# Pooled attention and a gated conv FFN: conv on two blocks without copies of h, keys loaded in pairs

## The chip, the cores and the metric

The kernel runs on one core of a Trainium2 chip. The metric is the device time of one launch in microseconds; beside it stands the profile of one execution. Engines are named as in the profile: PE (TensorE), PEld (its weight loads), DVE (VectorE), ACT (ScalarE), POOL (GpSimd), SP (SyncE, which only issues DMAs here).

## The reference

Eight batches b, each with 8 heads, 576 positions and head size 64. Keys and values are averaged over groups of 8 positions, so that each head attends to 72 pooled keys. The result feeds a feed-forward layer with a depthwise convolution over positions (3 taps) as a gate.

```
k_p = k.reshape(B, H, 72, 8, 64).mean(axis=3)         # v_p likewise
scores = q @ k_p.T / 8;  attn = softmax(scores)
x = (attn @ v_p) as (B, 576, 512)
h = max(x @ w_in, 0)                                  # (B, 576, 1024)
conv_out[s] = sum over k of conv_w[k] * h[s + k - 1]  # per channel, zeros outside
out = (h * sigmoid(conv_out)) @ w_out                 # (B, 576, 512)
```

## The kernel before

Batches go in four groups g of two. A group has 9 tiles t of 128 rows: four of its first batch, one shared (t = 4, 64 rows of each), four of the second.

Keys of a batch are loaded by `load_k` into one of three `kp` buffers, f32 in HBM and bf16 on the chip, with 9 neighbouring positions in a partition. `prep_k` pools and transposes them at once on PE: 36 matmuls against the pooling matrix `pm` (L469), or 72 in 64x64 tiles (L479); `copy_k` (L494) brings them to `kT`. q is transposed (L533, or L537 in 64x64 tiles) and copied to `qT` (L543). Values are loaded with 8 positions side by side in a partition; DVE adds halves three times (L503) and spreads the sum into `vm` times a head mask (L507).

A tile of attention is: scores (L585, or L572 in 64x64 tiles), row maximum on DVE (L598), the shift by it on PE (L618, first group) or DVE (L610, later groups, into `sd`), exp on ACT (L636), transposition to `eT` on PE (L647, copied at L661) or by DMA (L656, from the third group on), values (L672), quotient on DVE (L685, L687) to `x`, and transposition to `xT` on PE (L704, L712) or by DMA (L696, from batch 4 on).

The feed-forward part of a batch is: `w_in` (L738 by tiles for batch 0, L717 for the others), relu on ACT to `hT` (L748, L726), the convolution, tanh on ACT to `tg` (L815), `ffn_gate` on DVE (tg + 1 at L825, times h at L826, to `gT`), `w_out` on PE (L833), a copy to `osb` (L844) and two stores on SP's queue (L856).

The convolution is on PE as matmuls with diagonal 64x64 matrices `dw`, one for each tap, block of 128 channels `fb` and half of the block. To use all four 64x64 quarters of the array, row half r computes positions half r, and both output halves c are wanted of it. Where r and c differ, the data must lie in the other half of the partitions, so `ffn_swap` (L783) copies each pair of blocks of h with its halves exchanged into `hX`, on DVE or ACT, and `dw` holds the exchanged matrices too:

```
rhs=hT[r * D:(r + 1) * D, fb, src:src + hi - lo] if r == c
else hX[r * D:(r + 1) * D, fb % 2, src:src + hi - lo],
```

The order is not written by hand. `Graph` holds every step with an estimate of its duration on each engine that may do it, a key (a number that says how urgent it is), and the buffers that it uses; `Graph.order` plans all engines in time and emits the steps in the order of their planned starts. Each engine then runs its own instructions strictly in that order. PSUM's 8 banks are handed out in the plan, singly or in pairs. Loads are issued on POOL's queue, with at most eight in flight; the instruction that builds the identity `ident`, the pooling matrix `pm` and the head mask stand in the same queue. While PE would be idle, the plan puts in `fill` matmuls on a blank tile (L462).

Of the kernel before, what the change touches and what calls it, by code (L numbers as in the profile page):

```python
# [33 lines left out]
class Graph:  # L34
# [8 lines left out]
    STAY = 111.55  # L43
    LAZY = 1.11
# [5 lines left out]
    ATT = 39.8  # L50
    SPREAD = -183.35
    PREP_K = -29.07
    PREP_Q = 51.67
    PREP_V = 749.64
    GATE = 126.95
    CONV = 47.63
    SWAP = 261.14
    QCONV = -325.78
    OUT = 297.24
    LAST = 982.97  # L60
    FIRST = 196.4
    V0 = 281.91
    DW = 1007.11
# [3 lines left out]
    SWAP_DVE = 8  # L67
    BANKS = 8
    URGENT = -857.49
    NUDGE = {  # L70
        ('a', 0): -37.24, ('a', 1): 86.29, ('a', 2): -5.89, ('a', 3): -182.14, ('a', 4): -71.88, ('a', 5): -38.08,
        ('a', 6): -16.5, ('a', 7): 33.86, ('f', 0): -74.2, ('f', 1): -24.97, ('f', 2): -93.38, ('f', 3): 5.65,
        ('f', 4): 184.26, ('f', 5): -74.62, ('f', 6): -30.32, ('f', 7): -60.28, ('k', 0): 43.83, ('k', 1): -32.07,
        ('k', 2): 116.54, ('k', 3): 96.98, ('k', 4): 76.61, ('k', 5): 198.93, ('k', 6): -180.13, ('k', 7): 37.1,
        ('l', 'ident'): -61.73, ('l', 'k0'): -86.22, ('l', 'k0+'): -94.89, ('l', 'k1'): 2.95, ('l', 'k2'): 53.08, ('l', 'k3'): 66.15,
        ('l', 'mask'): -87.39, ('l', 'out'): 38.13, ('l', 'pm'): 4.15, ('l', 'q0'): -15.29, ('l', 'q0+'): 17.25, ('l', 'q1'): 12.42,
        ('l', 'q2'): 15.71, ('l', 'q3'): 88.03, ('l', 'v0'): -16.64, ('l', 'v1'): 37.82, ('l', 'v2'): -93.85, ('l', 'w0'): 36.34,
        ('l', 'w1'): 32.89, ('o', 0): 10.16, ('o', 1): -176.32, ('o', 2): 53.61, ('o', 3): 23.03, ('o', 4): -220.0,
        ('o', 5): -20.99, ('o', 6): -27.22, ('o', 7): 235.82, ('q', 0): -151.91, ('q', 1): 69.49, ('q', 2): -38.42,
        ('q', 3): 125.71, ('q', 4): 44.96, ('q', 5): 180.73, ('q', 6): 184.91, ('q', 7): 145.41, ('v', 0): -44.02,  # L80
        ('v', 1): -24.54, ('v', 2): 24.37, ('v', 3): 282.98, ('v', 4): -72.92, ('v', 5): -239.89, ('v', 6): -128.0,
        ('v', 7): -32.56,
# [14 lines left out]
    def order(self):  # L97
# [18 lines left out]
        def room(o):  # L116
            t, need = 0.0, 0
            new = {}
            for k in o.uses:
                if k.slots is not None:  # L120
                    continue
                if k.ring == "ps":
                    need += k.n
                    continue
                n = new[k.ring] = new.get(k.ring, 0) + 1
                q = taken[k.ring]
                if len(q) + n > self.rings[k.ring]:
                    f = idle_from(q[n - 1 - self.rings[k.ring]])
                    if f is None:
                        return None  # L130
                    t = max(t, f)
            if need:
                f = place(need)
                if f is None:
                    return None
                t = max(t, f[0])
            return t

        def place(n):
# [6 lines left out]
            return min(c, default=None)  # L146

# [32 lines left out]
        while avail:  # L180
# [56 lines left out]
            if o.land is not None:  # L237
                fixed, size, rate = o.land
                if size:
                    wire = max(wire, s + d + 0.3) + size / rate  # L240
                    o.end = wire + fixed
                    landings += [o.end] * o.dmas
                else:
# [24 lines left out]
def kernel(  # L268
# [17 lines left out]
    C = 9  # L286
# [14 lines left out]
             "hT": 2, "gT": 2, "xT": 2, "qT": 3, "kp": 3, "qp": 2, "hX": 3, "v": 2, "vm": 5, "kT": 5, "sd": 3, "r": 3, "s": 2}  # L301
# [8 lines left out]
    def banks(token):  # L310
# [6 lines left out]
    mask = const.tile([P, NJ, 3], BF16, name="mask")  # L317
    warm = const.tile([P, 2], FP32, name="warm")
# [3 lines left out]
    cw_raw = const.tile([3 * n_fb, 3 * D], FP32, name="cw_raw")  # L322
    convw = const.tile([P, 2, 3 * n_fb], FP32, name="convw")
    ident_2 = const.tile([P, D], BF16, name="ident_2")
    dw = const.tile([P, 2, 3 * n_fb, D], BF16, name="dw")
    shapes = {
        "qp": ([P, H // 2, S], BF16), "kp": ([P, H // 2, S], BF16), "qT": ([P, 2, 2, S], BF16),
# [4 lines left out]
        "hX": ([P, 2, S], BF16),  # L332
# [5 lines left out]
    def buf(*key):  # L338
        return buffers[key[0]][tokens[key].slots[0]]

# [17 lines left out]

    def load_q(b, **part):
        load_heads(buf("qp", b), q, b, **part)  # L360

    def load_k(b, **part):
        load_heads(buf("kp", b), k, b, **part)
# [9 lines left out]
    def load_conv():  # L373
        cw = moe_conv_w.rearrange("k (fb p) -> (k fb) p", p=P)
        nc.sync.dma_start(out=cw_raw[:, 0:P], in_=cw)
        nc.sync.dma_start(out=cw_raw[:, P:P + D], in_=cw[:, 0:D])
# [58 lines left out]

    def turn_conv_weights(ps):
        cps = bank(ps)[:, 0:6 * n_fb].rearrange("p (x j) -> p x j", x=2)
        for x in range(2):
            nc.tensor.transpose(
                out=cps[:, x, :],  # L440
                in_=cw_raw[:, x * D:x * D + P],
                identity=ident_f[0:3 * n_fb, 0:3 * n_fb],
            )

    def build_conv_matrices(part, ps=None, act=False):
        if part == 0:
            nc.vector.tensor_scalar(
                out=convw, in0=bank(ps)[:, 0:6 * n_fb].rearrange("p (x j) -> p x j", x=2), scalar1=2.0, scalar2=None, op0=OP.mult
# [3 lines left out]
        x, n = (part - 1) // 2, 3 * n_fb // 2  # L452
        todo = slice((part - 1) % 2 * n, (part - 1) % 2 * n + n)
        nc.vector.tensor_tensor(
            out=dw[:, x, todo],
            in0=ident_2.unsqueeze(1).to_broadcast([P, n, D]),
            in1=convw[:, x, todo].unsqueeze(2).to_broadcast([P, n, D]),
# [6 lines left out]
    def prep_k(b, half, ps, mode):  # L464
        for c in range(C):
            for hh in range(2):
                k_rows = buf("kp", b)[:, 2 * half + hh, c * D:(c + 1) * D]
# [30 lines left out]

    def prep_v(b, step):
        vt = buf("v", b)  # L500
        if step < 3:
# [8 lines left out]
            in1=mask.unsqueeze(3).to_broadcast([P, NJ, 3, D]),  # L510
# [271 lines left out]
    def ffn_swap(b, f2, r, copy):  # L782
        copy(  # L783
            out=buf("hX", b, f2)[r * D:(r + 1) * D, :, :],
            in_=buf("hT", b)[(1 - r) * D:(2 - r) * D, 2 * f2:2 * f2 + 2, :],
        )

    def ffn_conv(b, fb, ps):
        g, i = where[b]
        hT, hX = buf("hT", b), buf("hX", b, fb // 2)  # L790
        cps = banks(ps)
# [5 lines left out]
        for n in range(max(map(len, todo))):  # L797
            for r in range(2):
                for c in range(2):
                    if n >= len(todo[r]):  # L800
                        continue
                    tap, lo, hi, src = todo[r][n]
                    nc.tensor.matmul(  # L803
                        out=cps[c * D:(c + 1) * D, r, lo:hi],
                        lhsT=dw[r * D:(r + 1) * D, int(r != c), tap * n_fb + fb, :],
                        rhs=hT[r * D:(r + 1) * D, fb, src:src + hi - lo] if r == c
                        else hX[r * D:(r + 1) * D, fb % 2, src:src + hi - lo],
                        start=(n == 0),
                        stop=(n == len(todo[r]) - 1),
                        skip_group_check=True,  # L810
                    )
# [10 lines left out]
    def ffn_gate(b, fb):  # L822
        g, i = where[b]
        tg = buf("tg", b, fb)
        nc.vector.tensor_scalar(out=tg, in0=tg, scalar1=1.0, scalar2=None, op0=OP.add)  # L825
        nc.vector.tensor_tensor(  # L826
            out=buf("gT", g)[:, fb, i * S:(i + 1) * S], in0=tg, in1=buf("hT", b)[:, fb, :], op=OP.mult
        )
# [17 lines left out]
    def ffn_store(g, t, queue, only=None):  # L846
        osb = buf("osb", g, t)
        if t == 4:
            blocks = [(b, C - 1) for b in groups[g]]
        elif t < 4:  # L850
            blocks = [(groups[g][0], 2 * t), (groups[g][0], 2 * t + 1)]
        else:
            blocks = [(groups[g][1], 2 * t - 10), (groups[g][1], 2 * t - 9)]
        for j, (b, c) in enumerate(blocks):
            if only in (None, j):
                queue.dma_start(  # L856
                    out=out[b].rearrange("(p c) d -> c p d", c=C)[c],
                    in_=osb[j * TB:(j + 1) * TB, :],
                )
# [41 lines left out]
    kp, qp, qTt = {}, {}, {}  # L901
    kb = B and H * S * D * 4

    def add_load(kind, b, key, share=1.0, **part):
        f, ring, toks = (load_k, "kp", kp) if kind == "k" else (load_q, "qp", qp)
        if b not in toks:
            toks[b] = token(ring, b)
# [7 lines left out]
    def add_load_v(b, key):  # L915
# [6 lines left out]
             "k2", "q2", "v2", "k3", "q3"]  # L922
# [7 lines left out]
    cwl = add({"SP": 1.1}, soon(), load_conv, land=(1.5, 0, 1))  # L930
# [19 lines left out]
    hmc = add({"DVE": 0.5}, soon(), build_mask_columns, after=[hm])  # L950
    dw0 = add({"DVE": 0.2}, soon(), lambda: build_conv_matrices(0, cwtok), after=[cwp], uses=[cwtok])
    dwo = [add({"DVE": 1.0}, START + Graph.DW + n, lambda n=n: build_conv_matrices(n), after=[dw0]) for n in (1, 2, 3, 4)]
    win = [add({"POOL": 0.6}, first("w%d" % j), lambda j=j: load_w_in(j), land=(0.8, 2 * P * d_ff * 4, RATE)) for j in range(2)]
    wout = add({"POOL": 0.9}, first("out"), load_w_out, land=(LATE, d_ff * d_model * 4, RATE))
    for b in (1, 2, 3):
        add_load("k", b, first("k%d" % b))
        add_load("q", b, first("q%d" % b))
        add_load_v(b, first("v%d" % b) if b < 3 else -20)
    for b in range(4, B):
        w = (b - 4) * SLOTS  # L960
        add_load("k", b, w - 2)
        add_load("q", b, w - 1)
        add_load_v(b, w)
# [7 lines left out]

    def add_prep(b, key_k, key_q, gap):
        key_k, key_q = key_k + nudge("k", b), key_q + nudge("q", b)
# [220 lines left out]
```

## Time and profile before

| | us |
|---|---|
| median of 3 runs | 244.89 |
| lowest, highest | 244.22, 246.25 |
| profiled execution, span from first to last instruction | 244.0 |
| PE busy | 220.9 |
| PEld busy | 154.3 |
| DVE busy | 182.0 |
| ACT busy | 168.3 |
| POOL busy | 29.1 |

The profile is one execution; the span leaves out what lies before its first and after its last instruction. Busy time counts an engine once where its instructions overlap, so the sum over instructions of their mean duration is larger than the busy time. Matmuls overlap each other, and a matmul's own duration says little on the pace of many: the distance between neighbours does. A row of a group of instructions names line, engine, operation, tiles and shape, then the count, the busy time and the mean duration in ns, then idle time just before it and what ended it. A row of a stretch gives its bounds and length, the busy time and count of PE, PEld, DVE, ACT and POOL, the granted clock, the DMA share and GB/s. A row of the chain of waits gives start, duration and what ran.

### The profile page before, as it was taken

To read this page: it belongs to the slowest core of one execution; us is meant where nothing else is said; L and a number is where in the kernel's file an instruction comes from. 1 tells how busy PE (TensorE), PEld (TensorE's weight loads), DVE (VectorE), ACT (ScalarE), POOL (GpSimd) and SP (SyncE) were. 2 spreads that over 40 slices of the span, in tenths; PEclk is the share of its full clock that TensorE was granted. 3 is DMA by queue.
4 is the path that set the end of the run, shared out by engine and by line. 5 is a ranking of instruction groups with operands and counts; after the bars stand their busy time and mean duration, and the time that the engine had idled before them with its cause. 6 is when DMAs were issued, how large, how long until landed. Compare 5 with 4: busy or idle time off the path is not lost.

```text
span 244.0 us, 7852 instructions
## 1 busy us (share of the span) xinstructions
PE 220.9 (91%) x3354; PEld 154.3 (63%) x3377; DVE 182.0 (75%) x398; ACT 168.3 (69%) x264; POOL 29.1 (12%) x48
## 2 busy tenths in 40 slices
PE   6568998998999999999999996979999999899991
PEld 2446986876675676678775554757655576676440
DVE  7667648899999999999999995755799413956301
ACT  2254764599996876498998654949966386989330
POOL 7942223200122020220010000000000000000000
PEclk9999999999999999999999999999999999999998
DMA  5999999999189958697208568593216577400356
GB/s 81 164 205 207 207 208 208 207 207 202 22 141 185 197 83 190 104 179 153 46 3 141 126 134 91 107 139 89 24 46 149 109 137 167 117 3 6 84 137 164
DMA packets 43707, 31.53 MB, mean 129 GB/s; under 512 B 23680, under 2 KB 39064, under 8 KB 43672
## 3 DMA queue, kind: packets, MB, share of 16 engines
q0 software_dynamic: 15952, 16.26, 42.2%
q1 hardware_dynamic: 27640, 14.64, 29.5%
q8 instruction: 26, 0.43, 0.7%
q10 hardware_dynamic: 80, 0.13, 0.2%
q14 instruction: 9, 0.07, 0.1%
HBM read 32.52 MB, written 9.44 MB: 172 GB/s over the span
## 4 chain that ended last, share of the span: by engine, by line
PE 51%; DVE 26%; ACT 8%; DMA 7%; issue 5%; POOL 0%; SPq 0%; DVEq 0%; ACTq 0%; POOLq 0%
PE psum L833 16%; PE psum L717 14%; PE psum L803 7%; DVE negm L598 5%; DVE gT L826 4%; PE psum L672 3%; DVE sd L610 3%; DMA kp<-in_k_dram 3%; PE psum L738 3%; DVE tg L825 2%; ACT hT L726 2%; DVE hX L783 2%; DVE x L687 2%; DVE v L503 2%; DMA eT<-e 2%
## 5 line engine op out<-in xcount | busy, mean ns | idle before, releaser
L833 PE MATMUL psum<-w_out_sb,gT 128*128 128x512 bf16 x266 | 66.6, 379 | 2.0 <-issue 0.8
L717 PE MATMUL psum<-xT,w_in_sb 128*128 128x288 bf16 x448 | 61.1, 286 | 2.0 <-DMA xT<-x 1.3
L717 PEld LDWEIGHTS <-w_in_sb 128*128 128x128 bf16 x448 | 41.8, 98 | 15.4 <-DMA xT<-x 1.6
L833 PEld LDWEIGHTS <-gT 128*128 128x128 bf16 x288 | 26.0, 98 | 25.9 <-issue 0.7
L815 ACT ACTIVATE tg<-psum 128x576 bf16<-128x576 f32 x64 | 37.8, 655 | 3.0 <-PE psum L803 2.5
L726 ACT ACTIVATE hT<-psum 128x576 bf16<-128x576 f32 x56 | 34.4, 648 | 7.5 <-PE psum L717 7.1
L844 ACT COPY osb<-psum 128x512 f32<-128x512 f32 (+1 forms) x31 | 17.9, 579 | 24.5 <-PE psum L833 23.3
L783 DVE COPY hX<-hT 64x1152 bf16<-64x1152 bf16 x41 | 18.7, 458 | 18.3 <-ACT hT L726 15.4
L803 PE MATMUL psum<-hT,dw 64*64 64x224 bf16 (+3 forms) x576 | 30.9, 246 | 0.8 <-ACT tg L815 0.7
L803 PEld LDWEIGHTS <-dw 64*64 64x64 bf16 x1152 | 24.7, 107 | 10.5 <-issue 9.5
L826 DVE TENSOR_TENSOR gT<-tg,hT 128x576 bf16<-128x576 bf16 x64 | 29.3, 458 | 2.2
L803 PE MATMUL psum<-hX,dw 64*64 64x288 bf16 (+3 forms) x576 | 30.7, 246 | 0.0
L598 DVE TENSOR_REDUCE negm<-psum 128x8 f32<-128x576 f32 (+1 forms) x36 | 25.9, 750 | 2.4 <-PE psum L585 2.2
L783 ACT COPY hX<-hT 64x1152 bf16<-64x1152 bf16 x23 | 26.4, 1150 | 0.5
L687 DVE TENSOR_TENSOR x<-psum,r 128x512 bf16<-128x512 f32 x36 | 24.9, 692 | 1.2
L636 ACT ACTIVATE e<-sd 128x576 bf16<-128x576 f32 x27 | 18.2, 682 | 8.1 <-DVE sd L610 6.7
L672 PE MATMUL psum<-vm,eT 128*128 128x130 bf16 (+5 forms) x240 | 18.5, 222 | 4.2 <-DMA eT<-e 2.2
L825 DVE TENSOR_SCALAR tg<-tg 128x576 bf16<-128x576 bf16 x64 | 19.4, 304 | 3.4 <-ACT tg L815 3.2
L672 PEld LDWEIGHTS <-eT 128*128 128x128 bf16 (+1 forms) x240 | 14.7, 100 | 9.4 <-issue 3.0
L610 DVE TENSOR_TENSOR sd<-psum,negm 128x576 f32<-128x576 f32 x27 | 19.6, 749 | 0.1
L685 DVE RECIPROCAL r<-psum 128x8 f32<-128x8 f32 x36 | 7.3, 201 | 8.8 <-PE psum L672 8.7
L543 ACT COPY qT<-psum 128x1152 bf16<-128x1152 bf16 (+2 forms) x11 | 10.7, 992 | 4.2 <-PE psum L533 4.1
(67 smaller groups left out, 227.9 us busy)
## 6 DMA issues: line engine op xcount, KB each, us to landing
out_dram<-osb SPq DMA_DIRECT2D x71, 128.0 KB, 2.4
v<-in_v_dram POOLq DMA_DIRECT2D x8, 512.0 KB, 8.8
kp<-in_k_dram POOLq DMA_DIRECT2D x7, 576.0 KB, 16.0
qp<-in_q_dram POOLq DMA_DIRECT2D x7, 576.0 KB, 12.5
w_in_sb<-in_moe_w_in_dram POOLq DMA_DIRECT2D x2, 512.0 KB, 14.7
w_out_sb<-in_moe_w_out_dram POOLq DMA_DIRECT2D x1, 1024.0 KB, 20.0
kp<-in_k_dram POOLq DMA_DIRECT2D x2, 288.0 KB, 5.4
v<-in_v_dram POOLq DMA_DIRECT2D x8, 64.0 KB, 8.4
```

Of the source, the lines that this page charges most:

```text
L598: nc.vector.tensor_reduce(out=a["m"][0:rows], in_=a["s"][0:rows, :, 0:2 * KW].rearrange("p a (h s) -> p a h s", s=Sp), axis=AX.X, op=OP.ma ...
L610: nc.vector.tensor_tensor(out=a["d"][0:rows], in0=a["s"][0:rows, :, 0:2 * KW].rearrange("p a (h s) -> p a h s", s=Sp), in1=a["m"][0:rows]. ...
L672: nc.tensor.matmul(out=a["o"][lo:hi, h // 4, (h % 4) * (D + 1):(h % 4 + x1 - x0) * (D + 1)], lhsT=a["eT"][:, j, lo:hi], rhs=buf("vm", b)[: ...
L687: nc.vector.tensor_tensor(out=a["x"][0:rows].rearrange("p (a h d) -> p a h d", a=2, d=D), in0=ov[:, :, :, 0:D], in1=r[0:rows].unsqueeze(3) ...
L717: nc.tensor.matmul(out=banks(ps)[:, j, 0:SC], lhsT=w_in_block(dc, fb), rhs=buf("xT", g)[:, dc, i * S + j * SC:i * S + (j + 1) * SC], start ...
L726: nc.scalar.activation(out=buf("hT", b)[:, fb, :].rearrange("p (a s) -> p a s", a=2), in_=banks(ps)[:, :, 0:SC], func=ACT.Relu, scale=0.5,)
L783: copy(out=buf("hX", b, f2)[r * D:(r + 1) * D, :, :], in_=buf("hT", b)[(1 - r) * D:(2 - r) * D, 2 * f2:2 * f2 + 2, :],)
L803: nc.tensor.matmul(out=cps[c * D:(c + 1) * D, r, lo:hi], lhsT=dw[r * D:(r + 1) * D, int(r != c), tap * n_fb + fb, :], rhs=hT[r * D:(r + 1) ...
L815: nc.scalar.activation(out=tg.rearrange("p (a s) -> p a s", a=2), in_=banks(ps)[:, :, 0:SC], func=ACT.Tanh, scale=0.5,)
L825: nc.vector.tensor_scalar(out=tg, in0=tg, scalar1=1.0, scalar2=None, op0=OP.add)
L826: nc.vector.tensor_tensor(out=buf("gT", g)[:, fb, i * S:(i + 1) * S], in0=tg, in1=buf("hT", b)[:, fb, :], op=OP.mult)
L833: nc.tensor.matmul(out=bank(ps)[0:rows, :], lhsT=buf("gT", g)[:, fb, t * P:t * P + rows], rhs=w_out_sb[:, fb, :], start=(fb == 0), stop=(f ...
```

## The change

Convolution: one step now does two blocks `fb` = 2 f2 and 2 f2 + 1. Quarter (r, c) of the array works on block 2 f2 + (r ^ c), so all data come from `hT` as it lies; `hX`, `ffn_swap` and the exchanged half of `dw` are gone. Output half c of an odd block then holds the other half's channels, and the two halves change places when DVE adds 1 to tanh, in two instructions of 64 partitions. A step needs two pairs of PSUM banks at once (`two_pairs` in `Graph.order`).

Keys of batches 2 to 7: both batches of a group come by one load of 4608 neighbouring elements for each partition, DVE adds halves three times as for v, and 18 matmuls against a selection matrix `pick` transpose the sums of both batches. There is one buffer `kk` for keys, also for those of batches 0 and 1.

Stores: one DMA for each tile, except the last tile. The mask for `vm` is widened once to 64 equal columns. The conv weights need one load and one transposition, and two products instead of four. All keys of the plan (the constants of `Graph` and `NUDGE`) have other values, the loads at the start among them, so that the order of all engines' instructions is another one.

```
-             ... "qT": 3, "kp": 3, "qp": 2, "hX": 3, "v": 2, ...
+             ... "qT": 3, "kk": 1, "qp": 2, "v": 2, ...
...
-    dw = const.tile([P, 2, 3 * n_fb, D], BF16, name="dw")
+    dw = const.tile([P, 3 * n_fb, D], BF16, name="dw")
...
+    def load_pair(g):
+        rows = k[groups[g][0]:groups[g][1] + 1].rearrange("b h s d -> (b h s) d").rearrange("(p r) d -> p (r d)", p=P)
+        nc.gpsimd.dma_start(out=buf("kk", g).rearrange("p c x -> p (c x)"), in_=rows)
...
+    def widen_mask():
+        nc.vector.tensor_copy(out=mask_wide, in_=mask.unsqueeze(3).to_broadcast([P, NJ, 3, D]))
...
+    def pool_pair(g, step):
+        t, half = buf("kk", g), POOL * D >> step + 1
+        nc.vector.tensor_tensor(out=t[:, :, 0:half], in0=t[:, :, 0:half], in1=t[:, :, half:2 * half], op=OP.add)
+
+    def turn_pair(g, ps):
+        flat = banks(ps).rearrange("p a x -> p (a x)")
+        for c in range(C):
+            for hh in range(2):
+                nc.tensor.matmul(
+                    out=flat[hh * D:(hh + 1) * D, c * D:(c + 1) * D],
+                    lhsT=buf("kk", g)[:, c, 0:D],
+                    rhs=pick[:, hh],
+                    start=True, stop=True, skip_group_check=True,
+                )
+
+    def copy_pair(b, ps, hh, copy):
+        g, i = where[b]
+        part = slice(hh * D, (hh + 1) * D)
+        src = banks(ps).rearrange("p a x -> p (a x)")[part, 0:C * D].rearrange("p (c s j e) -> p s j e c", s=2, j=4, e=8)
+        copy(
+            out=buf("kT", b)[part, :, hh * Sp:(hh + 1) * Sp].rearrange("p j (e c) -> p j e c", c=C),
+            in_=src[:, i],
+        )
...
         nc.vector.tensor_tensor(
             out=buf("vm", b)[:, :, :, 0:D],
             in0=vt[:, :, 0:D].unsqueeze(2).to_broadcast([P, NJ, 3, D]),
-            in1=mask.unsqueeze(3).to_broadcast([P, NJ, 3, D]),
+            in1=mask_wide,
             op=OP.mult,
         )
...
-    def ffn_swap(b, f2, r, copy):
-        ...
-    def ffn_conv(b, fb, ps):
+    def ffn_conv(b, f2, pss):
...
+        for turn in range(2):
+            for n in range(max(map(len, todo))):
+                for r in range(2):
+                    j = r ^ turn
+                    if n >= len(todo[j]):
+                        continue
+                    tap, lo, hi, src = todo[j][n]
+                    for c in range(2):
+                        fb = 2 * f2 + (r ^ c)
+                        nc.tensor.matmul(
+                            out=banks(pss[r ^ c])[c * D:(c + 1) * D, j, lo:hi],
+                            lhsT=dw[r * D:(r + 1) * D, tap * n_fb + fb, :],
+                            rhs=hT[r * D:(r + 1) * D, fb, src:src + hi - lo],
+                            start=(n == 0), stop=(n == len(todo[j]) - 1), skip_group_check=True,
+                        )
...
     def ffn_gate(b, fb):
+        tg, gate = buf("tg", b, fb), buf("gT", g)[:, fb, i * S:(i + 1) * S]
+        if fb % 2:
+            for r in range(2):
+                nc.vector.tensor_scalar(
+                    out=gate[r * D:(r + 1) * D], in0=tg[(1 - r) * D:(2 - r) * D], scalar1=1.0, scalar2=None, op0=OP.add
+                )
+            tg = gate
+        else:
+            nc.vector.tensor_scalar(out=tg, in0=tg, scalar1=1.0, scalar2=None, op0=OP.add)
+        nc.vector.tensor_tensor(out=gate, in0=tg, in1=buf("hT", b)[:, fb, :], op=OP.mult)
...
     def ffn_store(g, t, queue, only=None):
...
+        queue.dma_start(out=rows, in_=osb)
```

The lines that the prediction names in the changed kernel: L787 is the `w_in` matmul by tiles (L738 before), L766 the other one (L717), L848 the convolution (L803), L882 `w_out` (L833), L871 the addition of 64 partitions, L556 the product with the mask (L507), L524 the pooling of keys and L530 their transposition.

The order in which POOL issues the loads at the start, by batch (q0 and k0 come in two parts; w_in in two halves):

```
before: k0, k0, (mask, ident,) q0, v0, (pm,) k1, rest of q0, q1, w_in 1, w_in 0, w_out, v1, k2, k3, q2 ...
after:  rest of q0, k0, q1, w_in 1, q0, (mask,) k0, v0, k1, w_in 0, (pm, ident,) w_out, v1, q2, q3, v2, pair 2/3 ...
```

## The prediction

> **What bounds the kernel now.** I read the page first, then the stretches, the groups of instructions, and the chain of waits. The page and the stretches:
>
> ```profile
> PE 220.9 (91%) x3354; PEld 154.3 (63%) x3377; DVE 182.0 (75%) x398; ACT 168.3 (69%) x264; POOL 29.1 (12%) x48
> ...
> 48.00:66.00 18.00, 16.30 (x383) 12.15 (x381) 17.32 (x39) 16.64 (x25) 0.00 (x0) 1.00 0.92 155
> 66.00:84.00 18.00, 17.44 (x331) 12.26 (x333) 17.56 (x36) 14.64 (x26) 3.51 (x5) 1.00 0.97 168
> 144.00:162.00 18.00, 14.72 (x184) 10.34 (x182) 13.35 (x31) 11.75 (x19) 0.00 (x0) 1.00 0.74 106
> 200.00:226.00 26.00, 24.84 (x412) 17.63 (x414) 15.68 (x40) 22.59 (x34) 0.00 (x0) 1.00 0.33 72
> ```
>
> PE is busy 91%, but from 48 to 144 us DVE is as full as PE, and in 48:66 ACT is too (16.64 of 18). So a change that lightens only one engine there gains little. The chain gives PE's real pace, since ends of matmuls overlap:
>
> ```profile
> 2.14 6.68 DMA kp<-in_k_dram
> 8.86 1.29 PE psum L469 x15
> ...
> 26.72 0.89 PE psum L738 x16
> ...
> 42.82 0.68 PE psum L469 x18
> ...
> 190.95 2.59 PE psum L833 x12
> 194.76 4.41 PE psum L717 x36
> ```
>
> Per matmul: L833 0.216 us, L717 0.1225, L738 0.056. With such steps for every line (conv L803: 18 in 0.40 us) I counted the work in both instruction orders: 207 us before, of which 9.9 stand ahead of the first L738 matmul (26.56 us). From there to PE's end (238.1) 197 us of work fill 211.5 us: 14.4 us are waits and changes of array shape (0.11 each: the timeline has the last L717 ahead of a conv 0.22 us before it, not 0.12). By the matmuls counted in each stretch 48:66 lost 3.6 us, 144:162 4.5, 200:226 2.7.
>
> **Part by part.** The groups with prices:
>
> ```profile
> L783 DVE COPY hX<-hT 64x1152 bf16<-64x1152 bf16 x41 | 18.7, 458 | 18.3 <-ACT hT L726 15.4 <-PE psum L803 2.0
> L783 ACT COPY hX<-hT 64x1152 bf16<-64x1152 bf16 x23 | 26.4, 1150 | 0.5
> L825 DVE TENSOR_SCALAR tg<-tg 128x576 bf16<-128x576 bf16 x64 | 19.4, 304 | 3.4 <-ACT tg L815 3.2
> L507 DVE TENSOR_TENSOR vm<-v,mask 128x960 bf16<-128x960 bf16 x8 | 9.2, 1156 | 0.2
> L503 DVE TENSOR_TENSOR v<-v 128x1280 bf16<-128x1280 bf16 x8 | 6.5, 818 | 0.2 <-DMA v<-in_v_dram 0.2
> L469 PE MATMUL psum<-pm,kp 128*64 128x144 bf16 x180 | 8.2, 247 | 3.6 <-DMA kp<-in_k_dram 3.6
> ```
>
> *Conv on pairs.* It removes 64 hX copies: 41 x 0.458 = 18.8 us of DVE, 23 x 1.15 = 26.4 of ACT. It adds 32 half-height additions for odd blocks, 32 x 0.304 = +9.7 of DVE: L783 itself shifts partitions at full pace, so I price a shifted 64x576 addition as a whole L825. Matmuls are unchanged: 1152, in runs of 32 or 40 a pair. A run takes four of eight banks; the next run then waits for two tanh (2 x 0.655), less than the 16 L717 (1.96 us) or 4 L833 plus a run (1.75) between most runs: 0.
>
> *Keys of 2 to 7.* Before: four batches in the wide form (36 matmuls at 0.033) and two in the narrow one (72 at 0.0115): 6.4 us of PE. After: 3 x 18 matmuls, not in the trace; nearest rows 0.022 (narrow L803) to 0.034 (L533): 1.2 to 1.8, I take 1.5. PE saves 4.9. The order also puts four halves of q in the narrow form instead of one (L533 18 in 0.62, L537 36 in 0.40): 0.6 more. PE: **-5.5**, bounds -5 to -6.2. DVE gains the pooling, by the slope of L503 (0.818 at 1280, 0.489 at 640): 1.34 + 0.75 + 0.46, three times: +7.7.
>
> *Wide mask.* L507 reads its mask at one value per 64; its 960 elements cost 1.156, an L503 of that size 0.65. Bounds 0.65 and 1.156; I take 0.65, whose operands it then shares in kind: 8 x 0.5 = -4.0 of DVE, and +1.2 once to widen the mask. Two fewer dw builds: -1.9. Copies of eT, xT, kT shift six or more from DVE to ACT: about -2 against +4. In all DVE -7, ACT -22.
> The Trainium skill, "VectorE: DVE Perf Modes" (Mode 2x_1P), asks for 4-byte alignment for two results a cycle, and a vm row is 65 elements of 2 bytes; "Vector Engine (DVE) Microarchitecture Reference" (5.1) says alignment makes no difference. By the first L507 stays near 1.16, by the second the sum stands; no row here decides it.
>
> *Stores and conv weights.* 35 tiles are stored by one DMA instead of two; in the chain one issue takes SP 0.54 us, and the page lands one in 2.4. They hide under matmuls; eT and xT sends queued behind them leave earlier, counted below. Last store: unchanged, 0.
>
> *The front.* The order of loads changes wholly. KB landed, in issue order before: k0 576, q0 832, v0 1408, k1 1984, q0+ 2304, q1 2880, w_in 3392, w_in 3904. v0 freed its queue slot at 12.98 and the second w_in let L738 start at 26.56: 186 KB/us. After: q0+ 320, half of k0 608, q1 1184, w_in 1696, q0 1952, rest of k0 2240, v0 2816, k1 3392, w_in 3904. So k0 is whole at 13.0 + (2240 - 1408)/186 = 17.5, against about 9 to 11; v0 at 20.6; w_in at 26.4 as before. POOL also moves pm and ident behind ten loads, two of which wait for a slot: ident about 13 us (4.1 before). PE's 13 fills (8 took 3.6 us before) end at 6.9, so it idles until 13.3. Then q0+ 1.3, k0 1.3, q0 1.06 after 16.5, q1 1.25 to 2.4, k0 0.65 to 1.3, copy 0.6, scores: the first row maximum starts at 20.8 to 22.5, against 13.48. From there DVE needs four maxima, v's sums, the mask product, a copy and three quotients, 8.4 us at 0.94 (gates in a row come every 0.715 us where the rows add to 0.762) = 7.9; PE turns x and ends k1, 0.9. The first w_in matmul (L787) at 29.6 to 31.3: **+3.7** with the same work behind PE. Bounds +1 (q1 and k0 overlap the chain) to +6 (k0's rest two us later).
> The doubled 1.3 is a row: L469's 18 matmuls took 1.29 us at 8.86 and 0.68 at 42.82. The Trainium skill, "TensorE: Matmul & The Clock Gate" (What's actually happening), halves the clock after one idle window of some 3.4 us. The trace agrees in the doubled time, not in the granted clock, which reads 1.00 there; by that rule a slow start follows the 6.4 us gap.
>
> *Stages with full ACT.* 48:66 lost 3.6 us, of which shape changes explain some 12 x 0.11 = 1.3; 200:226 lost 2.7, of them 1.8. With 22 us less ACT, and no hX between relu and conv, 2.3 and 0.9 can come back; in 144:162, where PE waited 2.2 us for an eT transposition, perhaps 1. Bounds 0 to -4.2; I take **-2.3**, the first stage alone, since DVE stays full: from the first conv to the last quotient of batch 3 the new order holds 45.7 us of DVE rows (x 0.94 = 43) beside 40 of PE plus some 4 of shape changes. Both orders change array shape 96 times.
>
> Sum: -5.5 + 3.7 - 2.3 = -4.1 us. The profiled span is 244.0; the median shown is 244.89, 0.9 more, which lies around the span and stays. Predicted **240.8 us**. A measurement of this kernel tells about 1% (2.4 us) from no change.
>
> **Rivals.**
> *More comes back (236 us).* All three stages recover (-4.2) and the front loses 1 to 2, as k0 and q1 overlap the DMA: -5.5 + 1.5 - 4.2 = -8.2. For: ACT falls furthest, and it is full where PE loses. Against: DVE's margin.
> *The front and DVE eat it (244 us).* DVE falls only 7 us; if the mask product stays at 1.156, five of the eight fall in its full stage, +2.5, and the front loses 4 to 5: -5.5 + 4.5 - 1 + 2 = 0. For: DVE at 17.56 of 18. By the alignment rule of the Trainium skill's "VectorE: DVE Perf Modes" (Mode 2x_1P) the product would stay there.
> *Pairs of keys arrive late (251 us, slower).* There is one kk buffer where kp had three; each pair's 1152 KB load waits for the previous pair's turn matmuls (L530), and DVE, in order, would stand before the pooling with v sums and quotients behind it, then PE. The first conv stands 18.0 us of PE work after the first L787, near 50.3. To the second pair's L530 are 32.3 us of PE work, 34.6 at 7% more, so the third pair is issued at 85.7 with POOL's 0.75; DVE has 48.8 us of rows before pooling it and reaches it at 50.3 + 48.8 x 0.94 = 96. The second pair: 64.4 and 78. Landing: 7.8 us (the lone q load at 126.83, 576 KB, used at 134.6) to 20.0 (w_out, 1024 KB among other loads). It decides from 11 us; at 17 us it costs 6.7 + 3.4 = 10. Against: the queues are nearly idle there (108:109 16 GB/s).
> *The change does less than it says*: if half-height additions cost more than 0.304, it is the second rival.
>
> **How the numbers follow.** Forecast 0.50, more comes back 0.18, eaten 0.19, late pairs 0.13. The forecast's own range, 237 to 243.5, lies above 242.4 (1%) with a tenth of its weight. Faster by over 1%: 0.45 + 0.18 = 0.63; within 1%: 0.05 + 0.18 = 0.23; slower: 0.13, and 0.01 of the eaten case. The range reaches to the faster rival's bound (-6.2 + 1 - 4.2, 235.5) and past the eaten case (+2): 235.0 to 247.0; late pairs stay outside.
>
> **What would show it.** Right: no hX; PE's L530 54 matmuls in 1.2 to 1.8 us; DVE about 175 busy, ACT about 146; L871 64 x 0.304; L556 at 0.65; first maximum near 21, first L787 near 30.3, first conv near 50; stretches around 50 to 70 with PE fuller. Wrong: L787 before 28 or after 32 (front), L556 near 1.16, DVE waiting for kk (late pairs), idle PE before conv runs (banks), or 144:162 as empty as now.

## The result, and the profile after

The changed kernel takes 323.08 us (median of 4 runs, 319.54 to 323.78) against 245.56 of the kernel before beside it: ratio 1.316, interval 1.3075 to 1.3254. The prediction was 240.8. The profiled execution has a span of 321.6 us, against 244.0. Where a median and a ratio below do not fit each other, it is because the ratio and its 95% interval leave out executions more than 1.5% above the fastest of the same kernel, which the median holds.

The page after: busy time by engine, then four rows of the 40 slices (PE busy, granted clock, DMA share, GB/s), the chain's shares by engine, and the row of the stores.

```profile
PE 227.5 (71%) x3181; PEld 154.4 (48%) x3206; DVE 177.1 (55%) x397; ACT 147.3 (46%) x245; POOL 26.2 (8%) x45
...
PE   7579989889924990099972886959686999994000
...
PEclk9699999999975896579996799988978999999555
DMA  7999999199492119522078999661798341112121
GB/s 109 198 205 207 214 206 165 17 172 192 81 182 71 51 55 117 77 51 51 17 66 73 126 172 103 60 45 32 68 86 94 98 62 41 53 53 80 51 80 39
...
DMA 38%; PE 31%; DVE 12%; issue 5%; ACT 5%; POOL 3%; SPq 1%; ACTq 0%; DVEq 0%; POOLq 0%
...
out_dram<-osb SPq DMA_DIRECT2D x35, 256.0 KB
```

DVE and ACT are as busy as forecast (about 175 and 146): the work was counted right. But the slices have holes, in which no engine works, and the chain (the work that ended last, followed back) is led by DMA, with 38% of the span against 7% in the page before. A slice is 8.04 us. In seven of them, six with PE at work and one after its end, the wires carry 51 to 55 GB/s; elsewhere they reach 214. The chain names what the kernel stands behind (start, duration, what):

```profile
74.01 26.22 DMA out_dram<-osb
...
119.17 17.39 DMA eT<-e
...
171.42 10.73 DMA eT<-e
...
276.23 27.41 DMA out_dram<-osb x2
```

SP's timeline shows why an eT transposition takes 17 us: the four sends stand behind six stores at which SP stood 37.14 us, 6.2 for each.

```profile
81.93 37.14 SPq L907 DMA_DIRECT2D out_dram<-osb  x6
119.17 19.55 SPq L705 DMA_TRANSPOSE eT<-e  x4
```

Three stretches (bounds and length, busy time and count of PE, PEld, DVE, ACT, POOL, granted clock, DMA share, GB/s):

```profile
126.00:132.00 6.00, 0.00 (x0) 0.00 (x0) 0.00 (x0) 0.00 (x0) 0.00 (x0) 0.50 1.48 64
270.00:290.00 20.00, 19.63 (x250) 11.58 (x251) 7.08 (x20) 11.65 (x20) 0.00 (x0) 1.00 0.14 53
294.00:318.00 24.00, 0.00 (x0) 0.00 (x0) 0.42 (x1) 1.03 (x3) 0.00 (x0) 0.57 0.21 70
```

From 270 to 290 hardly anything but stores moves: the DMA share is 0.14, about 2/16, at 53 GB/s. A tile of 256 KB then takes 262,144 B / 53 GB/s = 4.9 us. The 1.48 of 126:132 is no count of engines: it comes from two of the six us (128 to 130, 4.13, more than all 16 engines); from 130 to 132 it is 0.13 at 51 GB/s, the stores alone. In 294:318 PE is done and the kernel only waits for its last stores. The waits say the same: PE lost 35.7 us at L721 to eT, ACT 20.6 at L893 for a free `osb`.

```profile
PE psum L721 <- DMA eT<-e: 35.7, 8, 15.7
...
ACT osb L893 <- DMA out_dram<-osb: 20.6, 4, 11.1
```

The target of a store is now `rows[0, 2 * t:2 * t + 2]`, two rows of blocks by 64 positions by 512: 2 x 64 x 512, with two outermost. Before, each DMA had 64 x 512. In the four tiles t = 4 the two outer dimensions have one stride, so they can become 128; a burst of 244 GB/s at 296:297, among stores at 51, fits one such tile. Of the 35 tiles in one DMA 31 keep the two: 31 x 4.9 = 152 us on SP's queue, an estimate.

### The profile page after: what moved, and what is told of

It reads as the page before. It is cut to its first block, busy times and chain, and to the rows that moved or that the text cites. A ratio compares the mean times of both kernels' runs of the same rounds, so it can differ in the third digit from the quotient of the medians.

```text
span 321.6 us, 7449 instructions
## 1 busy us (share of the span) xinstructions
PE 227.5 (71%) x3181; PEld 154.4 (48%) x3206; DVE 177.1 (55%) x397; ACT 147.3 (46%) x245; POOL 26.2 (8%) x45
## 4 chain that ended last, share of the span: by engine, by line
DMA 38%; PE 31%; DVE 12%; issue 5%; ACT 5%; POOL 3%; SPq 1%; ACTq 0%; DVEq 0%; POOLq 0%
DMA out_dram<-osb 17%; DMA eT<-e 16%; PE psum L766 10%; PE psum L882 6%; PE psum L848 4%; DMA xT<-x 4%; PE psum L721 2%; DVE negm L647 2%; PE psum L787 2%; DVE gT L877 2%; DMA v<-in_v_dram 2%; PE psum L582 2%; DVE gT L871 2%; PE psum L634 2%; DVE sd L659 1%
## 5 line engine op out<-in xcount | busy, mean ns | idle before, releaser
L882 PE MATMUL psum<-w_out_sb,gT 128*128 128x512 bf16 x263 | 71.3, 401 | 3.1 <-issue 1.7
L766 PE MATMUL psum<-xT,w_in_sb 128*128 128x288 bf16 x448 | 64.3, 294 | 3.7 <-DMA xT<-x 2.9
L766 PEld LDWEIGHTS <-w_in_sb 128*128 128x128 bf16 x448 | 42.9, 100 | 18.7 <-issue 4.7
L721 PE MATMUL psum<-vm,eT 128*128 128x130 bf16 (+5 forms) x240 | 19.4, 233 | 36.2 <-DMA eT<-e 35.7
L893 ACT COPY osb<-psum 128x512 f32<-128x512 f32 (+1 forms) x31 | 18.0, 582 | 57.1 <-PE psum L882 26.9
L882 PEld LDWEIGHTS <-gT 128*128 128x128 bf16 x288 | 27.4, 102 | 28.5 <-issue 5.7
L721 PEld LDWEIGHTS <-eT 128*128 128x128 bf16 (+1 forms) x240 | 15.2, 105 | 42.1 <-DMA eT<-e 38.9
L848 PE MATMUL psum<-hT,dw 64*64 64x288 bf16 (+4 forms) x1152 | 30.9, 250 | 0.0
L848 PEld LDWEIGHTS <-dw 64*64 64x64 bf16 x1152 | 24.8, 109 | 10.3 <-issue 9.7
L876 DVE TENSOR_SCALAR tg<-tg 128x576 bf16<-128x576 bf16 x32 | 9.8, 307 | 29.8 <-ACT tg L859 29.8
L634 PE MATMUL psum<-kT,qT 128*128 128x144 bf16 (+1 forms) x136 | 13.3, 236 | 13.0 <-ACT osb L893 10.4
L871 DVE TENSOR_SCALAR gT<-tg 64x576 bf16<-64x576 bf16 x64 | 19.6, 306 | 1.2
L634 PEld LDWEIGHTS <-qT 128*128 128x128 bf16 (+1 forms) x136 | 9.6, 102 | 15.9 <-issue 14.3
L893 DVE COPY osb<-psum 128x512 f32<-128x512 f32 (+1 forms) x6 | 3.9, 644 | 22.2 <-DMA out_dram<-osb 18.9
L877 DVE TENSOR_TENSOR gT<-tg,hT 128x576 bf16<-128x576 bf16 x32 | 14.7, 459 | 1.1
## 6 DMA issues: line engine op xcount, KB each, us to landing
w_in_sb<-in_moe_w_in_dram POOLq DMA_DIRECT2D x2, 512.0 KB, 13.2
```

Source lines behind the costliest of these rows:

```text
L634: nc.tensor.matmul(out=heads[lo:hi, f], lhsT=buf("qT", b)[:, f, a, t % 5 * P:t % 5 * P + hi - lo], rhs=buf("kT", b)[:, 2 * f + a, :], star ...
L721: nc.tensor.matmul(out=a["o"][lo:hi, h // 4, (h % 4) * (D + 1):(h % 4 + x1 - x0) * (D + 1)], lhsT=a["eT"][:, j, lo:hi], rhs=buf("vm", b)[: ...
L766: nc.tensor.matmul(out=banks(ps)[:, j, 0:SC], lhsT=w_in_block(dc, fb), rhs=buf("xT", g)[:, dc, i * S + j * SC:i * S + (j + 1) * SC], start ...
L848: nc.tensor.matmul(out=banks(pss[r ^ c])[c * D:(c + 1) * D, j, lo:hi], lhsT=dw[r * D:(r + 1) * D, tap * n_fb + fb, :], rhs=hT[r * D:(r + 1 ...
L871: nc.vector.tensor_scalar(out=gate[r * D:(r + 1) * D], in0=tg[(1 - r) * D:(2 - r) * D], scalar1=1.0, scalar2=None, op0=OP.add)
L882: nc.tensor.matmul(out=bank(ps)[0:rows, :], lhsT=buf("gT", g)[:, fb, t * P:t * P + rows], rhs=w_out_sb[:, fb, :], start=(fb == 0), stop=(f ...
```

## Experiments

**First question: which part of the store.** Theory A: with two outermost, two of the 16 DMA engines carry the store. B: a single DMA of 256 KB is slow by its size. C: it is not the stores, but the new order or its loads.

*e1: two stores a tile in the changed kernel, all else as it is* (the edit shortened; `blocks` are the tile's two halves, as in the kernel before).

```
-        queue.dma_start(out=rows, in_=osb)
+        for j, (b, c) in enumerate(blocks):
+            queue.dma_start(out=out[b].rearrange("(p c) d -> c p d", c=C)[c], in_=osb[j * TB:(j + 1) * TB, :])
```

> The changed kernel with each tile stored by two DMAs of 64 rows again; all else, the order of the other engines too, stays. Theory A (a store whose outer dimension is 2 is carried by 2 of the 16 DMA engines: 51 to 54 GB/s when stores flow alone, 4.9 us for 256 KB, and the eT and xT sends wait behind them): 238 to 243 us. Rival B (one DMA of 256 KB is slow because of its size or because a whole osb buffer hangs on it): 238 to 243 too. Rival C (the new order or the single kk buffer makes the time, the waits for stores are a symptom): over 300.

Measured: 247.97 us against 244.24, ratio 1.0142 (1.0065 to 1.022). The stores cost 75 us, nearly the whole loss of 77.5; but the rest of the change is no gain, where 238 to 243 was expected. That is the second question.

*e2: the kernel before with the new store.*

```
-            queue.dma_start(out=out[b].rearrange("(p c) d -> c p d", c=C)[c], in_=osb[j * TB:(j + 1) * TB, :])
+        queue.dma_start(out=rows, in_=osb)
```

> The kernel before with this part alone: one DMA for each tile in place of two. A and B: 36 stores of 4.9 us are 176 us on two engines, the first at 68 us, and the transpositions among them: 290 to 330 us, flow of 51 to 54 GB/s after PE's end. C: 243 to 247.

Measured, in one execution: 324.69 us. The store alone does it, in the old order too. C falls.

*e3: two stores a tile again, but cut by columns, each 2 x 64 x 256.*

```
-        queue.dma_start(out=rows, in_=osb)
+        for x in range(2):
+            columns = slice(x * d_model // 2, (x + 1) * d_model // 2)
+            queue.dma_start(out=rows[..., columns], in_=osb[:, columns])
```

> The changed kernel with two DMAs for each tile as in e1, but cut by columns, so that each still has an outer dimension of 2 (2 x 64 rows x 256 columns, 128 KB). A: 310 us or more, since it is the outer dimension. B: about 240, since size and count are those of e1. C: over 300.

Measured, in one execution: 329.09 us. As many DMAs as before, of 128 KB each, and as slow as one: B falls. While its stores move alone (this run's stretch 270:290), the share is that of the changed kernel and the rate near it:

```profile
270.00:290.00 20.00, 20.00 (x263) 12.60 (x262) 7.07 (x20) 11.66 (x20) 0.00 (x0) 1.00 0.14 49
```

*e4 and e8: one DMA a tile with 16, or 4, outermost* (shortened). The rows of each group of batches are permuted in the output of both, to have such a target.

```
-        queue.dma_start(out=rows, in_=osb)
+        rows = out[groups[g][0]:groups[g][1] + 1].rearrange("b s d -> (b s) d")
+        rows = rows.rearrange("(x t y) d -> t x y d", x=16, y=8)[t]      # e8: x=4, y=32
+        queue.dma_start(out=rows, in_=osb)
```

> The changed kernel with one DMA for each tile, whose target is 16 blocks of 8 rows (rows of the output are permuted within a group; no arithmetic is changed). A: as e1, 237 to 243, with 35 DMAs of 256 KB landing in 2 to 4 us. B: over 310, since size and count are those of the changed kernel. C: over 300.

> One DMA for each tile with a target of 4 x 32 x 512 instead of 2 x 64 x 512 or 16 x 8 x 512 (the rows of each group are permuted in the output). Theory A, the number of DMA engines is the outermost count: four of them carry some 106 GB/s, a tile takes 2.4 us instead of 4.9, 36 stores hold them for 88 us in all; stores no longer fill the queue all the time, but eT and xT transpositions wait up to 2.4 us behind each: 254 us (249 to 270), a store alone at 106 GB/s. Rival A2, a threshold (only 16, or only as many rows as one DMA engine takes, is fast): over 300 us, as with two.

Measured: 248.24 us with 16 (ratio 1.013, 1.0036 to 1.0225; with e1's two stores 1.0142), 281.58 with 4 (1.1516). So one DMA of 256 KB with 16 outermost is as good as two of 128; where it moves alone the share reaches 0.93 at 291 GB/s (e4, 237.0:237.5), near all 16 engines. With 4 the share and the rate confirm A (e8's stretches with stores alone):

```profile
252.00:262.00 10.00, 10.00 (x48) 4.56 (x47) 2.50 (x7) 4.47 (x8) 0.00 (x0) 1.00 0.26 82
262.00:274.00 12.00, 1.16 (x6) 0.31 (x4) 0.42 (x1) 0.47 (x2) 0.00 (x0) 0.76 0.25 89
```

0.25 is 4/16, and 89 GB/s make 2.9 us of a tile. The time was missed by far, though: 254 was expected. I had added up the queue's load over the whole span, but behind a burst of stores stand the eT sends (in e8 four stores held SP for 15.45 us, from 87.11, and four sends for 17.33, from 105.17), and PE's next batch waits for them: 22.2 us in all, 11.7 at the longest. That bursts make the whole miss is not shown. No threshold either (A2 wanted over 300).

**Second question: why the rest does not gain.** PE work, counted as in the prediction, is 207 us before and 200.9 in e1, yet e1 is 3.7 us longer (1.6 to 5.4 by its interval; it has only four executions). Up to 92 us the two run level; then e1 falls back twice. The waits of e1 (total, times, longest) and its chain:

```profile
POOL v L387 <- DVE vm L556: 37.3, 5, 15.4
POOL kk L376 <- PE psum L530: 25.6, 2, 13.7
```

```profile
92.20 15.37 issue
...
108.35 6.84 DMA v<-in_v_dram
...
143.68 8.89 DMA xT<-x
```

POOL issues loads in order. The third pair of keys waits 13.7 us for the only `kk` buffer, and what is behind it in the queue waits too; a later v load waits another 15.4 us for its own buffer and lands at 115. The xT transpositions from 143.68 on meet the last q load, which also had to wait for its buffer. Each of the next kernels keeps the order of every engine's instructions and only gives a ring more buffers than the plan counts on (`HELD`), so that a load does not wait:

```
+    HELD = {"kk": 2}                      # e6: {"kk": 2, "v": 3}; e9: {"kk": 2, "qp": 3}
...
-                    k.slots = [len(taken[k.ring]) % self.rings[k.ring]]
+                    k.slots = [len(taken[k.ring]) % self.HELD.get(k.ring, self.rings[k.ring])]
```

> The kernel with two stores a tile, in which a second buffer holds keys; every engine keeps its order of instructions. The question is what the other parts lose, as this kernel without the buffer was 247.97 us beside 244.24 for before, while its PE work is 6 us less. Theory L, late loads: with one buffer the load of the third pair stood 13.7 us on POOL's queue for the turn (L530) of the second pair, landed at 96.0, DVE waited 1.93 us for it and PE 1.64 at L530, and the v loads queued behind it were late in turn (PE work fell 4.3 us behind that of before from 92 to 124). The second buffer takes that wait away: 245.5 us (244 to 246.8). Rival M: DVE and the DMA engines are full there, the load lands earlier and something else ends last: 247 to 248.5.

> As the kernel with a second buffer of keys, and a third one for v, in which the v loads don't wait for the mask product (L556) of two batches before: POOL stood 37.3 us for it, 15.4 of them up to 107.59, whose load then held DVE for 1.17 us and PE for 0.92 at 115. Theory L: 1 us less than with the second buffer of keys alone, 244.5 us (243 to 246). Rival M: no less, 246 to 248.5, as one v load of 576 KB moved ahead lands on the same DMA engines as the stores and the eT transpositions.

> Two stores a tile, two buffers of keys, and a third one for q; all engines keep their order. With two buffers of keys alone it was 1.0059 of before, and PE still waited 4 us for xT transpositions that took 8 to 9 us to land (from 138.8 in the kernel with a third v): the last q load, 576 KB, is issued at 140, when its buffer comes free, into the eT and xT transpositions of batch 6. Theory Q, the collision: with a third buffer it leaves at about 91, the xT step falls to 3.5 to 5 us and the time by 2 to 3.5 us: 242.8 us (241.5 to 244.3). Rival: the transpositions and the stores fill the DMA engines there by themselves (0.59 MB of load are only a fifth of the 3.07 MB that moved from 132 to 152 us), and the time falls by less than 1 us: 245 to 246.

Measured: e5 246.0 us (ratio 1.0059, 1.0027 to 1.0091), e6 244.28 (0.9949, 0.9909 to 0.9988), e9 244.34 (0.9996, 0.9966 to 1.0027). The step from e1 to e5 has the sign and size of theory L, but the intervals overlap, and e7 below, which keeps one `kk` buffer and whose front did not move, is at 1.005 (1.010 by the medians): a gain from the second buffer alone is not shown, though PE's idle time at L530 falls from 2.1 us to 0.5. With it the two later v loads leave only 0.9 and 3.1 us earlier, since they still wait for their own buffers. The third v after it is clear, 1.1% or 2.7 us, nearly three times what was expected. The third q (e9 against e5) is worth 0.6%, 1.5 us, with intervals that just touch: less than the 2 to 3.5 expected and more than the rival's "under 1". Its mechanism shows in the rows of the `w_in` matmul, e5 first (there the chain has an xT step of 8.84 us at 140.33), then e9: the idle time before it, its last column, is gone. But the values (L721) now wait longer, 4.6 us instead of 1.6.

```profile
L766 PE MATMUL psum<-xT,w_in_sb 128*128 128x288 bf16 x448 | 62.0, 288 | 4.3 <-DMA xT<-x 4.1
```

```profile
L766 PE MATMUL psum<-xT,w_in_sb 128*128 128x288 bf16 x448 | 61.6, 286 | 0.2
...
L721 PE MATMUL psum<-vm,eT 128*128 128x130 bf16 (+5 forms) x240 | 18.0, 222 | 4.6 <-DVE gT L877 2.2 <-DMA eT<-e 2.1 <-DVE vm L556 0.2
```

The last q load left at 106.12 and not at about 91: on POOL's queue it stood behind a v load that waited 13.2 us for its buffer. With the xT wait goes a stretch of slow clock: in 144:162 the granted clock is 0.91 in e1, e5 and e6, and 1.00 in e9.

*e7 and e10: the front.* e7 is e1 with POOL's first steps in another order; e10 is e6 with that order and q1's transposition behind the first two scores.

```
+        # POOL: q0+ k0 ident q0 k0+ mask pm q1 v0 w0 k1 w1    (was: q0+ k0 q1 w0 q0 mask k0+ v0 k1 w1 pm ident)
+        # e10 also: [PE q1 half 0, ACT copy, PE q1 half 1] behind the second scores, DVE copy behind the second maximum
```

> The kernel with two stores a tile and other places of the first loads on POOL alone: identity after the second load (it stood at 11.7 us behind ten), q0's second part and k0's rest ahead of q1, v0 and w_in. q1 lands last of what the first scores stand behind, 1728 KB at about 186 KB/us, 13.5 us instead of 16.1. The first row maximum at 16.8 instead of 19.46, the first w_in matmul at 26.4 instead of 29.0. If the front still costs what my prediction put down for it (+3.7), the time falls by about 2.5 us, to 245.5 (244.5 to 246.5). The rival: the front's lag was caught up by 60 us already (PE work there 39.1 us against 38.8 before), as DVE and ACT set the pace behind it, and the time stays within 0.7 us, 247.3 to 248.5.

> Two stores a tile, two buffers of keys, three of v, POOL's first loads in the other order (identity third, q0 and k0 first), and q1's transposition moved behind the first two scores on PE, its copies behind them on ACT and DVE. Without the last two it was 0.9949 of before (243.2 us beside 244.46). In the kernel with the other order of loads alone q1 landed at 14.86 and k0's rest waited behind it on PE in order, so that the first row maximum stayed near 19.5. Now the first scores stand behind 1152 KB and not 1728: row maximum at 12.5 to 14, v's sums when v0 lands (17 to 18), the first w_in matmul at 25 to 26.5 instead of 29. Theory F, the front is worth what my prediction put down: 2.5 us less, 240.8 (239.5 to 242). Rival: caught up behind it, where DVE and ACT set the pace: 242.5 to 243.5.

Measured: e7 246.87 us (1.005, 1.0018 to 1.0083), which cannot be told from e1. Its ratio lies where a moved front was expected, but the front did not move: the first row maximum starts at 19.46 as in e1, the first `w_in` matmul at 29.75 (29.0 in e1). q1's transposition stood before k0's on PE, in order, and PE waited for q1 until 14.86. So e7 is in effect a second measurement of e1.

```profile
14.86 2.13 PE L582 MATMUL psum<-ident,qp 128*64 128x128 bf16 x36 [4.01 <-DMA qp<-in_q_dram]
```

e10 takes 241.9 us (0.9903, 0.9869 to 0.9936). Here the front does move: the first row maximum at 13.98 (19.4 in the changed kernel), the first `w_in` matmul at 25.45 (28.95). Of these 3.5 us 0.5% is left at the end, 1.1 us against e6, with intervals that overlap: nearer to "caught up" than to "worth what I put down".

```profile
13.98 1.42 DVE L647 TENSOR_REDUCE negm<-psum 128x8 bf16<-128x576 f32 x2 [0.73 <-PE psum L634]
```

*e12: e6 with the mask product from the narrow mask again.*

```
-            in1=mask_wide,
+            in1=mask.unsqueeze(3).to_broadcast([P, NJ, 3, D]),
```

> Two stores a tile, two buffers of keys, three of v, and the mask product (L556) again from the narrow mask: 1.156 us instead of 0.653, eight times. The prediction counted that five of these lie where DVE is full and cost 2.5 us: 245.7 us (244.7 to 246.5), against 0.9949 of before, 243.2, with the wide mask. The rival: DVE has slack of that size in its stage now, and the time rises by less than 0.8 us.

Measured: 248.46 us, 1.0193 (1.0163 to 1.0224). That is 2.4% above e6, some 6 us by the ratios (3.3 between the two profiled executions, 245.9 and 242.6), for 8 x 0.50 = 4.0 us of DVE:

```profile
L556 DVE TENSOR_TENSOR vm<-v,mask 128x960 bf16<-128x960 bf16 x8 | 9.2, 1153 | 0.1
```

So a microsecond of DVE at these eight places costs 0.8 us or more at the end: the time is above the 244.7 to 246.5 that were expected, and the slack of the rival theory is not there.

*e13: three v, three q, one `kk`, and the early start.*

> Two stores a tile, one buffer of keys, three of v and three of q, and the early start (three of each of the three do not fit into SBUF). If the late loads and the front add up: v alone is worth 2.7 us beside the second keys, q 2 to 3.5, the front 2.5, while the late third pair stays (-2 not had): 247.5 - 2.7 - 2.7 - 2.5 = 239.6 us (238.5 to 242). If they overlap, so that DVE and ACT set the pace, 242 to 244.

Measured: 240.39 us against 244.46, ratio 0.9843 (0.9816 to 0.9869). This is below both kernels, by 1.6% of before. It lies near the 240.8 that was predicted for another kernel, which is luck. What is left of the late loads is the third pair: PE still idles 1.6 us at L530 in it.

```profile
L530 PE MATMUL psum<-pick,kk 128*64 128x64 bf16 x54 | 1.4, 197 | 1.6 <-DVE kk L524 1.6
```

## Why the prediction was wrong, point by point

**Stores: the step that failed.** "35 tiles are stored by one DMA instead of two; in the chain one issue takes SP 0.54 us, and the page lands one in 2.4. They hide under matmuls" put the part at 0. It measured +75 us (e1 against the changed kernel). The 2.4 us are the landing of a 64 x 512 store, as the page before has it, and I carried them over to a store of another shape, which takes 4.9 us on the wires alone.

```profile
out_dram<-osb SPq DMA_DIRECT2D x71, 128.0 KB, 2.4
```

The trace of before had no row for the new shape, so by the prediction's own rule it needed bounds from both sides, and the rivals needed a store that lands late; I gave neither, since one DMA for two looked like less work. The half sentence "eT and xT sends queued behind them leave earlier" had the right queue and the wrong sign.
The Trainium skill, "DMA: Bandwidth & Descriptors" (Why a DMA increments its semaphore by 16 and not by 1), says that a DMA runs on the largest number of engines up to 16 that divides the slowest dimension (above 1) of both sides. The runs agree: a DMA share of 0.14 with two outermost, 0.25 to 0.26 with four, up to 0.93 with 16. It spoke against this change, and the prediction did not weigh it.

**Keys: right.** L530 has 54 matmuls busy 1.4 us in all (1.2 to 1.8 said). The counted PE work falls by 6.1 us, against 5.5.

**Wide mask and additions: right in price, too small in worth.** The rows of the changed kernel:

```profile
L871 DVE TENSOR_SCALAR gT<-tg 64x576 bf16<-64x576 bf16 x64 | 19.6, 306 | 1.2
...
L556 DVE TENSOR_TENSOR vm<-v,mask_wide 128x960 bf16<-128x960 bf16 x8 | 5.2, 653 | 0.1
```

0.306 and 0.653 us stand for 0.304 and 0.65. The output rows of L556 begin every 130 bytes, and still it takes what the slope of L503 gives. That sides with the Trainium skill's "Vector Engine (DVE) Microarchitecture Reference" (5.1) and against "VectorE: DVE Perf Modes" (Mode 2x_1P). But I priced the mask at 2.5 us of the end, and e12 gives 3.3 to 6. The terms for DVE add up to -8.1, not to the -7 that I wrote; e1 measures -6.2 (175.8 against 182.0).

**Front: the delay is there, the size too large.** The first maximum at 19.4 (20.8 to 22.5 said) and the first L787 at 28.95 (29.6 to 31.3 said) were a little earlier than the bounds. The price +3.7 took it that all of the lag stays; e10 has back 3.5 us of it at L787 and 1.1 at the end. So some two thirds of the late start were caught up behind it, if e10's 0.5% holds.

**Stages with full ACT: less than said.** The -2.3 were for the first stage, 48:66, alone. In e1 the PE work done in 48:66 rises from 14.7 to 15.4 us, in 66:84 from 16.8 to 17.1, in 200:226 from 23.7 to 24.6: 0.7 us in the first, 1.9 in all three (counted a little higher than in the prediction, whose losses make 14.4 and 23.3 for before). Of this 0.9 is lost again in 144:162 (13.7 to 12.8), at the xT transpositions: "144:162 as empty as now" was one of my signs of being wrong, and it came.

**Late loads: the rival that I kept too narrow.** I wrote "pairs of keys arrive late" with a landing from which it decides, 11 us, and gave it 0.13. In e1 the third pair landed 11.2 us after its issue, and DVE waited 1.9 us for it, as that working has it. What I left out is that the q and v rings wait on their own buffers in the same way, on the same queue: the third v gave 2.7 us, the third q 1.5. From e1 to e6 the loads cost 4.7 us (1.9% of ratio), counted from e7 only 1.0%. Without the stores the change should have been 240.8, or 238.2 with the front at the 1.1 us that e10 gives it. e1 is 247.97, and e7's ratio makes 245.5. Of these 9.8 or 7.3 us the loads make about 6.2 or 3.9, more than half; the rest is not accounted for.

What stays open: how much of e12's 2.4% is beyond the 4.0 us of DVE; what the second buffer of keys is worth, as e1's interval is wide; and how far the parts add up in e13. From e1's 1.0142, less 1.1% for v, 0.6% for q and 0.5% for the front, they give 0.992; from e7's 1.005 they give 0.983, and 0.984 was measured. So the difference may lie in e1's four executions; no run settles it.

## What to carry to other kernels

Merging two DMAs into one changes the shape, not only the count: look at the outermost dimension of the target (here 16 and 64 were fast, 2 and 4 slow), and price a shape that the trace does not show by bounds, however harmless it looks. The DMA share in a stretch where one kind of transfer moves alone tells how many engines carry it (0.14 of 16 is two); where kinds mix it does not. On an in-order load queue a load that waits for its buffer delays every load behind it, so memory given back by a change (here `hX`) is best spent on the rings whose loads wait: here v and q, more than keys.

## What the runs showed of the hardware

Rate by outermost count of a store on SP's queue: 49 to 53 GB/s with 2, 82 to 89 with 4, up to 291 for half a microsecond with 16, which in the kernel's time is no different from two stores with 64. The size of one DMA (128 or 256 KB) made no difference. In the holes the granted clock drops to 0.50 (126:132) and stays there for some us when PE works again (104:106, PE busy throughout), so the 75 us hold some slow matmuls too: PE's busy time is 227.5 us against 220.2 in e1, whose program differs in the stores alone.
